# A gated feed-forward kernel behind a light convolution: the convolution laid on other steps, two of its taps moved from ScalarE and GpSimd to VectorE

## The chip, the cores and the metric

The kernel runs on one core of a Trainium2 chip. The metric is the device time of one execution in microseconds, as the median of several executions. All times below that belong to one place in the program come from one profiled execution.

## What is computed

The input x has 8 sequences of 4096 tokens with 192 channels. A causal convolution of 7 taps runs over the tokens; its weights are a softmax over the taps, one row for each of 8 groups of 24 channels. A feed-forward layer of width 2048 follows.

```
w   = softmax(weight)                     # 8 x 7, one row per group of 24 channels
y[t]= sum_k w[group, k] * x[t + k - 6]    # zeros ahead of a sequence
h   = y @ w_in                            # 32768 x 2048
g   = h            where h >= 1
      0            where h <= -1
      (h+1)^2 / 4  between
out = g @ w_out                           # 32768 x 192
```

Everything is float32. The kernel gets that precision from matmuls on values split into a high and a low part.

## The kernel before, in words

**Tiles.** The 32768 tokens are cut into 64 groups of TB = 512. A group goes through NPAIR = 8 steps, and a step handles two of the 16 slices of 128 hidden channels. So there are 512 steps q. Two groups, the tokens "a" (even group) and "b" (odd group), make a pair c; the 16 steps of a pair are called a block here, and i is the number of a step in its block. Steps 0 to 7 multiply a's tokens, 8 to 15 b's. Names: T is a transpose, R the rest.

**A step.** TensorE runs mm1(q), 18 matmuls that make h of this step, and then mm2(q-3), 18 matmuls that add g of three steps earlier into the four banks accm and accr. ScalarE makes relu and square (L570, L571) of h of this step and later the cast gh of the step before (L581). VectorE makes gl = g - gh of two steps before (L587), the sum m of gl's halves (L593), and g = max(h, min(g, 1)) of this step (L901), which frees h. h has two buffers, so mm1(q) needs g of q-2 to be done. Every eighth step, i = 2 and i = 10, ScalarE copies the four banks out (L617); GpSimd issues DMAs that add them up in the next two steps, and VectorE transposes the result (L639) in i = 7 and 8, and in 15 and 0.

**The convolution of the next groups runs beside this.** It works on three units: "a" (the first 128 channels of a's tokens), "b" (the same of b's), and "r", the rest (the last 64 channels of both). Each is loaded, transposed on VectorE (T, L164), and summed over taps 0 to 6. Method `taps` makes tap 0 on ScalarE and each later tap as a product on ScalarE (L238) and an addition on GpSimd (L249); `taps_dve` makes each as one fused operation of VectorE (L233). Before, only a uses `taps_dve` in the steady part. Then the unit is split into hi (a cast on ScalarE) and lo = y - hi: `split` subtracts on GpSimd (L280), `split_rest` on VectorE (L291). DMAs of SyncE's queue make copies of hi and lo with the halves of the partitions exchanged.

**What sets the order.** All engines run their queues in the order in which the program was written. The tables PLAN_B, PLAN_A and PLAN_R say in which step i which taps of a unit are written. The additions of GpSimd and its subtraction are held (`held`, `fresh`) and written one step after their product, with a dependency on the sum m of that step. mm1 of steps 0 to 7 reads a's hi and lo, that of steps 8 to 15 b's; r's are read in all 16. The blocks 0 and 1 have plans of their own (FIRST_A and the like; SECOND_B).

Of the kernel before, what the change touches and what calls it, by code (L numbers as in the profile page):

```python
# [8 lines left out]
F32 = mybir.dt.float32  # L9
# [22 lines left out]
def lightconv_then_ffn(ctx: ExitStack, tc: tile.TileContext, x, weight, w_in, w_out, out):  # L32
# [24 lines left out]
    nc = tc.nc  # L57
# [90 lines left out]
    class Conv:  # L148
# [137 lines left out]
        def split_rest(self):  # L286

            hi = xo.tile([P, TB], F32R, name="rh", bufs=2)
            lo = xo.tile([P, TB], F32R, name="rl", bufs=2)
            nc.scalar.copy(hi, self.y)  # L290
            nc.vector.tensor_sub(lo, self.y, hi.bitcast(F32))  # L291
            for key, t in (("hi", hi), ("lo", lo)):
                w = self.swapped(t, "r" + key, 2)
                xop[2 * self.c]["r", key] = (t[TOP], w[BOT])
                xop[2 * self.c + 1]["r", key] = (w[TOP], t[BOT])

        def split_halves(self):


            n = self.n  # L300
            y, late = self.y[:, 0:n], slice(n, TB)
            t, w = (act.tile([P, 2, TB], F32R, name=n, bufs=3) for n in ("gh", "gl"))
            t32, w32 = t.bitcast(F32), w.bitcast(F32)
            nc.scalar.copy(t[:, 0, 0:n], y)
            nc.vector.tensor_sub(t[:, 1, 0:n], y, t32[:, 0, 0:n])
            for to, half in ((t32[TOP, :, late], BOT), (w32[BOT, :, late], BOT),
                             (w32[BOT, :, 0:n], TOP)):
                nc.sync.dma_start(out=to, in_=t32[half, :, 0:n])
            for i, key in enumerate(("hi", "lo")):
                xop[2 * self.c + 1]["r", key] = (t[TOP, i], w[BOT, i])  # L310
# [497 lines left out]
    def whole(j, *cols):  # L808
        for _ in chunks[j].bits(*cols):
# [25 lines left out]

    PLAN_B = {12: ("T",), 14: (0, 1), 15: (2,), 0: (3,), 1: (4,), 2: (5,), 3: (6,), 5: "split"}
    PLAN_A = {1: ("T",), 2: (0,), 4: (1,), 6: (2,), 7: (3,), 9: (4,), 10: (5,), 11: (6,),
              12: "split"}  # L840
    PLAN_R = {2: ("T",), 4: (0,), 6: (1,), 7: (2,), 8: (3,), 9: (4,), 10: (5,), 11: (6,),
              13: "split"}
    SECOND_B = {0: (0, 1), 1: (2,), 2: (3,), 3: (4,), 4: (5, 6), 5: "split"}


# [5 lines left out]
    def conv_slot(i, b, a, r, turns=None):  # L851
        early = b is not None and b.c == 0
        plans = ((None if early else b, SECOND_B if b and b.c == 1 else PLAN_B),
                 (a, FIRST_A if early else PLAN_A),
                 (r, FIRST_R if early else PLAN_R))
        for u, plan in plans:
            what = plan.get(i, ()) if u else ()
            if turns is not None and turns != ("T" in what):
                continue
            if what == "split":  # L860
                if u is r:
                    u.split_rest()
                else:
                    u.split()
                continue
            if "T" in what:
                u.transpose()
            ks = [k for k in what if k != "T"]
            if ks:
                (u.taps_dve if u is a and not early else u.taps)(*ks)  # L870

# [60 lines left out]
    def first_step(q):  # L934
# [38 lines left out]
        if q > 6:  # L973
            advance(b, b)
        conv_slot(q, conv_b, conv_n.get("a"), conv_n.get("r"))

    conv_n, ahead = {}, {}
    for q in range(NQ + LATE):
# [10 lines left out]
        if c == 0 and i in (4, 5, 10):  # L989
            u = {4: "a", 5: "r", 10: "b"}[i]  # L990
# [18 lines left out]
        elif q < NF32:  # L1009
# [10 lines left out]
            act_max(q)  # L1020
            parts_lo(q, (False,))
            conv_slot(i, conv_b, conv_n.get("a"), conv_n.get("r"))
            if j >= NPAIR - 2:
                store(0, "mr"[j - NPAIR + 2])
        else:
# [17 lines left out]
            if q < NQ:  # L1043
                units = conv_b if i < 8 else conv_n.get("b"), conv_n.get("a"), conv_n.get("r")
                conv_slot(i, *units, turns=False)
# [55 lines left out]
```

## Time and profile before

| | |
|---|---|
| median of 3 runs | 2065.69 us (2064.97 to 2066.06) |
| the profiled execution | 2064.92 us |
| its span, first to last instruction | 2063.1 us |
| busy share of the span: TensorE, ScalarE, VectorE, GpSimd | 100%, 95%, 91%, 38% |
| granted TensorE clock, mean | 1.0 of full speed |

The busy share adds up the time in which at least one instruction of an engine was running; the ends of matmuls in it are modelled. A wait is shown in brackets behind the instruction that came after it, with the engine and line that ended it. A time from start to start of two neighbours on an engine is what the first one costs there; it can be shorter than the first one's own time, since they overlap.

### The profile page before, as it was taken

How to read it: one execution, taken by the hardware profiler on the slowest of the kernel's cores; microseconds unless marked ns; L12 is line 12 of the kernel's file. 1: busy time of each engine (PE TensorE's matmuls, PEld its weight loads, DVE VectorE, ACT ScalarE, POOL GpSimd, SP SyncE). 2: the span in 40 equal slices, each digit the busy share in tenths (PEclk: the TensorE clock that was granted, in tenths of full speed). 3: DMA queues.
4: the chain of work that ended last, by engine and by line, in shares of the span. 5: the costliest groups of instructions: out<-in, count | busy, mean ns of one | idle time of the engine just before them, and what ended most of it. 6: DMA issues, size and time to landing. Idle time of an engine off the chain costs nothing.

```text
span 2063.1 us, 46868 instructions
## 1 busy us (share of the span) xinstructions
PE 2054.3 (100%) x18644; PEld 1841.6 (89%) x18644; DVE 1871.6 (91%) x2109; ACT 1962.2 (95%) x2381; POOL 785.3 (38%) x749
## 2 busy tenths in 40 slices
PE   9999999999999999999999999999999999999999
PEld 6989889998899998888989998889899889998898
DVE  8898998999989999899899898998989989999988
ACT  7799999999999999999999999999999999999997
POOL 1534343343443433434434334344333343443431
PEclk9999999999999999999999999999999999999999
DMA  6333333443444434334333344343443433434323
GB/s 177 79 64 66 70 73 71 82 75 56 79 71 76 77 61 82 66 71 85 64 72 71 72 82 74 57 79 67 79 75 60 84 65 71 83 64 73 70 55 55
DMA packets 470685, 152.27 MB, mean 74 GB/s; under 512 B 418944, under 2 KB 426624, under 8 KB 470464
## 3 DMA queue, kind: packets, MB, share of 16 engines
q1 hardware_dynamic: 446880, 109.17, 25.9%
q0 software_dynamic: 23424, 39.99, 13.5%
q8 instruction: 146, 2.39, 0.5%
q14 instruction: 75, 0.61, 0.1%
q10 hardware_dynamic: 160, 0.10, 0.0%
HBM read 32.84 MB, written 25.17 MB: 28 GB/s over the span
## 4 chain that ended last, share of the span: by engine, by line
PE 67%; ACT 14%; DVE 9%; issue 4%; DMA 3%; POOL 2%; SPq 1%; ACTq 0%; DVEq 0%; POOLq 0%
PE h L483 34%; PE accr L536 20%; PE accm L536 10%; DVE gl L587 5%; ACT gh L581 4%; DMA lo<-lo 3%; ACT p L238 3%; ACT g L570 3%; ACT t L617 2%; POOL lo L280 2%; DVE g L901 2%; DVE y L233 1%; DVE m L593 1%; PE accm L503 1%; PE accr L503 1%
## 5 line engine op out<-in xcount | busy, mean ns | idle before, releaser
L587 DVE TENSOR_TENSOR gl<-g,gh 128x1024 fp32r<-128x1024 f32 x495 | 634.9, 1283 | 118.5 <-ACT gh L581 113.9
L536 PE MATMUL accr<-gh,wg 64*128 64x512 f32 x3960 | 635.9, 377 | 0.0
L483 PE MATMUL h<-hi,w 64*128 64x512 f32 x4032 | 634.2, 379 | 0.1
L901 DVE SCALAR_TENSOR_TENSOR g<-g,h 128x1024 f32<-128x1024 f32 x504 | 605.9, 1202 | 5.1 <-ACT g L571 3.0
L570 ACT ACTIVATE g<-h 128x1024 f32<-128x1024 f32 (+1 forms) x497 | 507.1, 1020 | 57.2 <-PE h L483 57.1
L571 ACT ACTIVATE g<-g 128x1024 f32<-128x1024 f32 (+1 forms) x497 | 525.8, 1058 | 15.8
L581 ACT CAST gh<-g 128x1024 fp32r<-128x1024 f32 x495 | 512.5, 1035 | 0.5 <-DVE g L901 0.4
L483 PEld LDWEIGHTS h<-hi,w 64*128 64x128 f32 x4032 | 418.6, 186 | 47.5 <-DVE g L901 12.5
L536 PEld LDWEIGHTS accr<-gh,wg 64*128 64x128 f32 x3960 | 406.5, 185 | 38.1
L483 PE MATMUL h<-lo,w 64*128 64x512 f32 x2016 | 435.1, 379 | 4.5 <-DMA lo<-lo 2.2
L249 POOL TENSOR_TENSOR y<-y,p 128x512 f32<-128x512 f32 x180 | 231.3, 1285 | 522.4 <-DVE m L593 269.0
L536 PE MATMUL accr<-gl,words 64*128 64x512 f32 x1980 | 419.0, 376 | 0.0
L249 POOL TENSOR_TENSOR r<-r,p 128x512 f32<-128x512 f32 x180 | 231.7, 1287 | 459.6 <-DVE m L593 269.5
L593 DVE TENSOR_TENSOR m<-gl 128x512 fp32r<-128x512 f32 x495 | 340.2, 687 | 26.7 <-PE h L483 0.5
L536 PE MATMUL accm<-gh,wg 64*128 64x512 f32 x1980 | 318.3, 376 | 0.0
L483 PE MATMUL h<-rhi,w 64*128 64x512 f32 x992 | 296.6, 379 | 0.0
L483 PE MATMUL h<-rh,w 64*128 64x512 f32 x992 | 293.6, 376 | 0.0
L483 PEld LDWEIGHTS h<-lo,w 64*128 64x128 f32 x2016 | 231.7, 186 | 40.1 <-DMA lo<-lo 24.5
L536 PEld LDWEIGHTS accr<-gl,words 64*128 64x128 f32 x1980 | 230.2, 186 | 16.2
L536 PEld LDWEIGHTS accm<-gh,wg 64*128 64x128 f32 x1980 | 215.2, 186 | 16.3
L627 POOL DMA_DIRECT2D t<-t x244 | 206.6, 983 | 31.3 <-ACT t L617 16.3
L536 PE MATMUL accm<-m,words 64*128 64x512 f32 x990 | 213.9, 382 | 0.0
(161 smaller groups left out, 2320.4 us busy)
## 6 DMA issues: line engine op xcount, KB each, us to landing
t<-t POOLq DMA_DIRECT2D x183, 128.0 KB, 3.6
out_dram<-osb SPq DMA_DIRECT2D x366, 64.0 KB, 1.9
raw<-in_x_dram SPq DMA_DIRECT2D x334, 68.0 KB, 2.6
hi<-hi SPq DMA_DIRECT2D x128, 128.0 KB, 3.1
lo<-lo SPq DMA_DIRECT2D x126, 128.0 KB, 2.3
t<-t POOLq DMA_DIRECT2D x61, 256.0 KB, 3.3
rhi<-rh SPq DMA_DIRECT2D x62, 128.0 KB, 3.1
rlo<-rl SPq DMA_DIRECT2D x62, 128.0 KB, 2.3
```

The costliest lines, as they stand in the source:

```text
L238: nc.scalar.mul(p, self.xT[:, SH + k:SH + k + TB], wk[:, self.wsel, k:k + 1])
L249: fresh.append(lambda p=self.product(k): nc.gpsimd.tensor_add(y, y, p))
L280: sub = eng.tensor_sub(lo, self.y, hi.bitcast(F32))
L483: nc.tensor.matmul(h[e], w[HALVES[e], c0:c0 + P], seen(x[e][e]), start=(n == 0), stop=(n == len(mms) - 1))
L536: mm = nc.tensor.matmul(accs[s][bank], w[half], in_turn(g[half]), start=(j == 0 and bank not in seen), stop=(j == NPAIR - 1 and k % 3 == 2 ...
L570: nc.scalar.activation(g[:, e, :], hs[q][:, e, :], AF.Relu, bias=0.5, scale=0.5)
L571: nc.scalar.activation(g[:, e, :], g[:, e, :], AF.Square)
L581: nc.scalar.copy(gh[:, e, :], gs[q][:, e, :])
L587: nc.vector.tensor_sub(gl[:, e, :], g[:, e, :], gh[:, e, :])
L593: return nc.vector.tensor_add(gt, gl[:, 0, :], gl[:, 1, :])
L627: nc.gpsimd.dma_start(out=to, in_=src, accum_op=ALU.add)
L901: nc.vector.scalar_tensor_tensor(out=g, in0=g, scalar=1.0, in1=h, op0=ALU.min, op1=ALU.max)
```

## The change

The three plans are laid out anew. The products and casts of ScalarE are taken off the steps 2 and 10, in which it copies the banks; B is transposed in step 10 and split in 3 (was 12 and 5), A is split in 11 (was 12), its taps 1 to 6 stand in steps 3 to 8 (were 4, 6, 7, 9, 10, 11). The rest's taps 5 and 6 become fused operations of VectorE in steps 9 and 10, and its split is written in two steps: the cast and hi's DMAs in step 12, the subtraction and lo's DMAs in step 13.

```diff
             nc.scalar.copy(hi, self.y)
-            nc.vector.tensor_sub(lo, self.y, hi.bitcast(F32))
             for key, t in (("hi", hi), ("lo", lo)):
+                if key == "lo":
+                    nc.vector.tensor_sub(lo, self.y, hi.bitcast(F32))
                 w = self.swapped(t, "r" + key, 2)
                 xop[2 * self.c]["r", key] = (t[TOP], w[BOT])
                 xop[2 * self.c + 1]["r", key] = (w[TOP], t[BOT])
+                yield
...
-    PLAN_B = {12: ("T",), 14: (0, 1), 15: (2,), 0: (3,), 1: (4,), 2: (5,), 3: (6,), 5: "split"}
+    PLAN_B = {10: ("T",), 11: (0,), 12: (1,), 13: (2,), 14: (3,), 15: (4,), 0: (5,), 1: (6,),
+              3: "split"}
...
+            if what in ("hi", "lo"):
+                if what == "hi":
+                    u.parts = u.split_rest()
+                next(u.parts)
+                continue
...
-                (u.taps_dve if u is a and not early else u.taps)(*ks)
+                dve = not early and (u is a or u is r and ks[0] > 4)
+                (u.taps_dve if dve else u.taps)(*ks)
```

VectorE's queue in the middle of a block, steps 9 and 10. Before, where y is a's sum and r the rest's tile:

```order
L587 TENSOR_TENSOR gl<-g,gh 128x1024
L233 SCALAR_TENSOR_TENSOR y<-xT,wk,y 128x512
L593 TENSOR_TENSOR m<-gl 128x512
L901 SCALAR_TENSOR_TENSOR g<-g,h 128x1024
L587 TENSOR_TENSOR gl<-g,gh 128x1024
L233 SCALAR_TENSOR_TENSOR y<-xT,wk,y 128x512
L593 TENSOR_TENSOR m<-gl 128x512
L901 SCALAR_TENSOR_TENSOR g<-g,h 128x1024
```

And of the changed kernel in the same two steps:

```order
L589 TENSOR_TENSOR gl<-g,gh 128x1024
L233 SCALAR_TENSOR_TENSOR r<-r,wk 128x512
L595 TENSOR_TENSOR m<-gl 128x512
L910 SCALAR_TENSOR_TENSOR g<-g,h 128x1024
L589 TENSOR_TENSOR gl<-g,gh 128x1024
L233 SCALAR_TENSOR_TENSOR r<-r,wk 128x512
L595 TENSOR_TENSOR m<-gl 128x512
L164 STREAM_TRANSPOSE xT<-raw 128x544
L910 SCALAR_TENSOR_TENSOR g<-g,h 128x1024
```

The taps in these steps are the rest's now, a's have moved ahead of them, and B's transpose has come from step 12 into step 10.

ScalarE's queue in steps 11 to 13, right behind the copies of the banks. Before:

```order
L570 ACTIVATE g<-h 128x1024
L571 ACTIVATE g<-g 128x1024
L238 ACTIVATE p<-r,wk 128x512
L581 CAST gh<-g 128x1024
L570 ACTIVATE g<-h 128x1024
L571 ACTIVATE g<-g 128x1024
L275 CAST hi_14028<-y 128x512
L581 CAST gh<-g 128x1024
L570 ACTIVATE g<-h 128x1024
L571 ACTIVATE g<-g 128x1024
L290 CAST rh<-r 128x512
L581 CAST gh<-g 128x1024
```

Of the changed kernel, steps 11 and 12 and the start of 13:

```order
L572 ACTIVATE g<-h 128x1024
L573 ACTIVATE g<-g 128x1024
L245 ACTIVATE y<-xT,wk 128x512
L275 CAST hi_13926<-y 128x512
L583 CAST gh<-g 128x1024
L572 ACTIVATE g<-h 128x1024
L573 ACTIVATE g<-g 128x1024
L238 ACTIVATE p<-xT,wk 128x512
L290 CAST rh<-r 128x512
L583 CAST gh<-g 128x1024
L572 ACTIVATE g<-h 128x1024
```

The casts hi of A and rh of the rest have come a step nearer to the copies, and stand with B's first two taps. VectorE's subtraction rl stays in step 13.

GpSimd's queue from the rest's first addition to B's last. Before:

```order
L249 TENSOR_TENSOR r<-r,p 128x512 x5
L627 DMA t<-t 128x512
L627 DMA t<-t 64x512
L249 TENSOR_TENSOR r<-r,p 128x512
L627 DMA t<-t 64x512 x2
L280 TENSOR_TENSOR lo_1862<-y,hi_1861 128x512
L249 TENSOR_TENSOR y<-y,p 128x512 x5
L627 DMA t<-t 128x512
L627 DMA t<-t 64x512
L249 TENSOR_TENSOR y<-y,p 128x512
L627 DMA t<-t 64x512 x2
L280 TENSOR_TENSOR lo_2388<-y,hi_2387 128x512
```

Of the changed kernel:

```order
L249 TENSOR_TENSOR r<-r,p 128x512 x4
L629 DMA t<-t 128x512
L629 DMA t<-t 64x512
L280 TENSOR_TENSOR lo_1812<-y,hi_1811 128x512
L629 DMA t<-t 64x512 x2
L249 TENSOR_TENSOR y<-y,p 128x512 x6
L629 DMA t<-t 128x512
L629 DMA t<-t 64x512
L280 TENSOR_TENSOR lo_2280<-y,hi_2279 128x512
L629 DMA t<-t 64x512 x2
```

The rest has four additions instead of six, and each subtraction lo now stands between the two halves of the DMAs that add up the banks.

## Rows read from the trace of the kernel before

**Rows 1.** Page, part 1: busy time of each engine, share of the span, instructions.

```profile
PE 2054.3 (100%) x18644; PEld 1841.6 (89%) x18644; DVE 1871.6 (91%) x2109; ACT 1962.2 (95%) x2381; POOL 785.3 (38%) x749
```

**Rows 2.** Chain of waits, last block: start, length, work; first and last of 16.

```profile
1989.93 1.94 PE h L483 x18
...
2048.20 1.83 PE h L483 x12
```

**Rows 3.** Timeline of TensorE, first mm1 of two successive blocks: start, length, instructions.

```profile
909.56 0.59 PE L483 MATMUL h<-hi,w 64*128 64x512 f32 x4
...
973.06 0.59 PE L483 MATMUL h<-hi,w 64*128 64x512 f32 x4
```

**Rows 4.** Timeline, step 8 of that block, with GpSimd's subtraction in step 6.

```profile
938.35 1.28 POOL L280 TENSOR_TENSOR lo<-y,hi 128x512 fp32r<-128x512 f32 x1 [4.02 <-ACT p L238]
...
940.64 0.59 PE L483 MATMUL h<-hi,w 64*128 64x512 f32 x4
...
942.49 0.18 PEld L483 LDWEIGHTS h<-lo,w 64*128 64x128 f32 x1 [0.44 <-DMA lo<-lo]
...
945.29 0.70 PE L483 MATMUL h<-hi,w 64*128 64x512 f32 x4
```

**Rows 5.** List of waits: who waited for whom, us in total, times, longest.

```profile
DVE rl L291 <- ACT rh L290: 25.7, 31, 1.0
PEld h L483 <- DMA lo<-lo: 24.5, 59, 0.5
```

**Rows 6.** Timeline, steps 13 to 15 of the block before that one.

```profile
902.46 0.60 ACT L290 CAST rh<-r 128x512 fp32r<-128x512 f32 x1
...
902.96 1.04 ACT L581 CAST gh<-g 128x1024 fp32r<-128x1024 f32 x1
...
903.09 0.69 DVE L291 TENSOR_TENSOR rl<-r,rh 128x512 fp32r<-128x512 f32 x1 [0.82 <-ACT rh L290]
...
903.70 0.69 DVE L593 TENSOR_TENSOR m<-gl 128x512 fp32r<-128x512 f32 x1
...
904.44 0.19 PEld L536 LDWEIGHTS accm<-m,words 64*128 64x128 f32 x2 [0.34 <-DVE m L593]
...
905.57 0.30 PEld L483 LDWEIGHTS h<-hi,w 64*128 64x128 f32 x4 [0.40 <-DVE g L901]
```

**Rows 7.** Timeline of ScalarE, step 2 and the start of step 3.

```profile
919.48 1.03 ACT L570 ACTIVATE g<-h 128x1024 f32<-128x1024 f32 x1 [0.23 <-PE h L483]
...
921.50 1.05 ACT L617 COPY t<-accr 128x512 f32<-128x512 f32 x2
...
923.40 0.75 ACT L238 ACTIVATE p<-xT,wk 128x512 f32<-128x512 f32 x1
924.03 1.05 ACT L581 CAST gh<-g 128x1024 fp32r<-128x1024 f32 x1
924.96 1.04 ACT L570 ACTIVATE g<-h 128x1024 f32<-128x1024 f32 x1
```

**Rows 8.** Timeline of VectorE, steps 6, 7 and 12, and mm1 of step 14.

```profile
935.72 1.23 DVE L587 TENSOR_TENSOR gl<-g,gh 128x1024 fp32r<-128x1024 f32 x1
936.86 0.75 DVE L233 SCALAR_TENSOR_TENSOR y<-xT,wk,y 128x512 f32<-128x512 f32 x1
937.53 0.68 DVE L593 TENSOR_TENSOR m<-gl 128x512 fp32r<-128x512 f32 x1
938.13 1.22 DVE L901 SCALAR_TENSOR_TENSOR g<-g,h 128x1024 f32<-128x1024 f32 x1
939.28 1.43 DVE L587 TENSOR_TENSOR gl<-g,gh 128x1024 fp32r<-128x1024 f32 x1
...
962.80 0.74 DVE L164 STREAM_TRANSPOSE xT<-raw 128x544 f32<-128x544 f32 x1
963.46 1.18 DVE L901 SCALAR_TENSOR_TENSOR g<-g,h 128x1024 f32<-128x1024 f32 x1
...
964.72 0.70 PE L483 MATMUL h<-hi,w 64*128 64x512 f32 x4
```

More of the change, by code (lines that the diff above doesn't have):

```diff
@@ L833, in lightconv_then_ffn @@
     whole(2, 0, CI)
-    PLAN_B = {12: ("T",), 14: (0, 1), 15: (2,), 0: (3,), 1: (4,), 2: (5,), 3: (6,), 5: "split"}
[L839 to L842, printed above, removed]
+    PLAN_B = {10: ("T",), 11: (0,), 12: (1,), 13: (2,), 14: (3,), 15: (4,), 0: (5,), 1: (6,),
+              3: "split"}
+    PLAN_A = {1: ("T",), 2: (0,), 3: (1,), 4: (2,), 5: (3,), 6: (4,), 7: (5,), 8: (6,), 11: "split"}
+    PLAN_R = {2: ("T",), 3: (0,), 4: (1,), 5: (2,), 6: (3,), 7: (4,), 9: (5,), 10: (6,), 12: "hi",
+              13: "lo"}
     SECOND_B = {0: (0, 1), 1: (2,), 2: (3,), 3: (4,), 4: (5, 6), 5: "split"}
@@ L859, in conv_slot @@
                 continue
+            if what in ("hi", "lo"):
[3 more added lines that the diff above has]
+                continue
             if what == "split":
                 if u is r:
-                    u.split_rest()
+                    for _ in u.split_rest():
+                        pass
                 else:
```

## The prediction, made before the changed kernel was run

> **What bounds the kernel now.** TensorE is busy for 100% of the span, ScalarE 95%, VectorE 91%, GpSimd 38% [rows 1]. That share does not say whether TensorE waits, since the ends of its matmuls are modelled, so I read its pace instead. In the last block of 16 steps, which has nearly no convolution, the chain of waits is TensorE alone; from its first mm1 to its sixteenth it takes 58.27 us, which is 3.885 us a step [rows 2]. That is what the 36 matmuls of a step need, and the change leaves them alone: sixteen steps cannot take less than 62.16 us. A block in the middle takes 973.06 - 909.56 = 63.50 us [rows 3], so each of the 29 blocks 2 to 30 (alike within 0.4 us) loses 1.34 us, 38.9 us in all. This is what a better order can win.
>
> Where a block loses it: (a) **Step 8** takes 945.29 - 940.64 = 4.65 us, 0.77 too many; TensorE waits for the DMA that lands lo of the tokens B [rows 4]. Its source is GpSimd's subtraction in step 6, from the split that PLAN_B puts in step 5. The list of waits has this wait 59 times, two a block [rows 5]. (b) **Steps 14 and 15** lose the other 0.57. In step 13 VectorE stands 0.82 us before rl, because ScalarE's cast rh is still to come; the sum m and the maximum g stand behind rl in its queue. TensorE then waits 0.34 for m, and later 0.40 until g is made and h is free [rows 6]. The wait for rh occurs 31 times [rows 5].
>
> **Taking (a) away.** B's split moves from step 5 to step 3, its subtraction from 6 to 4: two paces, 7.77 us, earlier, where 0.77 are missing. With T(n) for the start of mm1 of step n, it starts at about T(4)+6.05 (0.8 after m, as in [rows 4, 8]), and with the 2.9 us from its end to the weight load that it lets go [rows 4] its data are there more than 5 us before step 8 reads them. Gain 29 x 0.77 = 22.3 us. A's split goes from 12 to 11, which only adds slack.
>
> **Taking (b) away.** The cast of the rest's hi stands in step 12 and the subtraction in 13, so VectorE finds rh made; y of the rest is complete in step 10. Gain 29 x 0.57 = 16.6 us, if nothing else makes VectorE late there.
>
> **ScalarE.** From start to start, relu and square cost 2.02 us, the four copies of an evacuation 1.90, a product 0.63, the cast gh 0.93 [rows 7], a cast of one half 0.50 [rows 6]. A step without extras is 2.95, which is 0.93 under the pace. Before, steps 2 and 10 hold copies and a product, 1.60 over. Now they hold the copies alone: 0.97 behind. Step 11 (cast, first tap) and step 12 (cast, product) lose 0.20 each, so it is 1.37 behind at worst; the five steps 13 to 1, one product each, give 0.30 back apiece, which just fits before step 2. After step 2 it is 0.97 behind, after step 3 1.17, and back on pace in step 7. A block has two products fewer, 2 x 0.63 = 1.26 us, and ScalarE needs 60.1 in it (16 x 2.95 + 12 x 0.63 + 3 x 0.50 + 2 x 1.90). That wins nothing by itself, since TensorE is the bound; it keeps the lag under the old one. GpSimd loses two additions of 1.28 a block, and nobody waits for them.
>
> **VectorE is where a price may stand.** From start to start a fused tap takes 0.67 us, gl 1.14, m 0.60, g 1.15, a transpose 0.66 [rows 8]; a step with a tap is 3.56. It gets two taps more a block (2 x 0.67 x 30 = 40 us of work), and since A's taps are moved together and R's stand behind them, each of the steps 3 to 10 has a tap, and 7, 8 and 10 a transpose too. Additions of the rest in steps 5 and 6, and B's subtraction in 4, run into the next gl: it took 1.43 instead of 1.23 with GpSimd's lo beside its start [rows 4, 8], so 0.20 more in steps 5, 6 and 7. In step 4 gl starts 3.44 after T(4), when ScalarE's cast of step 3 is done (relu at 2.15 after T, that is 919.48 less 909.56 + 2 x 3.885 [rows 3, 7]; 0.97 late; + 2.02 + 1.13, a cast of 1.03, 0.02, - 3.885). From there VectorE has no gap. Start of gl after T: step 5 3.14, step 6 3.02, step 7 2.89, step 8 3.40, step 9 3.70, step 10 3.38. End of g after T: step 8 3.40 + 1.14 + 0.67 + 0.60 + 0.63 + 1.21 = 7.65 (the half transpose put at 0.63), step 10 3.38 + 1.14 + 0.67 + 0.60 + 0.66 + 1.21 = 7.66. The limit is two paces less 0.08, 7.69: g frees the h that mm1 wants two steps on, and in step 12 of before g ended at 964.64 and that mm1 started at 964.72 [rows 8]. So the stretch ends with 0.03 us to spare, by a sum of ten terms. Steps 11 to 15 hold few extras and bring VectorE back. I take 0.1 us a block lost here (30 x 0.1 = 3 us), between 0 and 0.5 (15 us; 0.5 is 0.1 more on each of five taps). Below zero it can't go, since TensorE sets the pace.
>
> **The rest.** Block 1 keeps SECOND_B, so its steps 3 to 5 hold B's taps and now R0, R1, R2 besides, and ScalarE comes out about 1 us later than now: once, between 0 and 3 us; I take 2. R's tap in step 9 has a new wait, on GpSimd's last addition. That one starts at T(8)+5.9 to 6.1, ends by T(8)+7.4, and the tap is due at T(8)+8.7; behind it stand m and g of step 9. It costs nothing while those 1.3 us last. B's transpose in step 10 reads data that were loaded in step 0.
>
> **Sum.** The profiled execution's 2064.92 (span 2063.1 and 1.8 around it) - 38.9 + 3 + 2 = 2031.0; the median of the runs lies 0.8 above it: 2031.8, said as 2032.
>
> **Rivals.** *VectorE becomes the bound of steps 3 to 10.* For it speaks the margin of 0.03 us; against it, that a step with a tap (3.56, or 3.76 beside GpSimd) is still under the pace. If each of the three meetings with GpSimd cost the whole 0.35 us that its subtraction had left when gl began [rows 4, 8], and not 0.20, a block would lose 0.45 more: 2032 + 30 x 0.4 = 2044. The Trainium skill has such a rule: its page "SBUF — State Buffer", section "Who interferes with whom", says that a VectorE instruction with two SBUF inputs is blocked fully behind a GpSimd one that started first. By that rule the time is this rival's; the row agrees that gl is held up, but shows 0.20 of the 0.35. Chance 0.18.
>
> *Only the first stall goes.* If VectorE is still late in step 13, (b) stays: 2032 + 16.6 = 2048. For it speaks that gl there waits for ScalarE's cast of step 12, which now has two operations ahead of it; against it, that m would end at T(13)+6.1 (3.64 + 1.14 + 0.6 + 0.7), where it ended at 7.06 (904.39, and T(13) = 964.72 - 63.50 - 3.885). Chance 0.10.
>
> *Slower.* If R's tap in step 9 waits for GpSimd, VectorE's queue stands behind it. Were that addition a whole step late (3.885), each block would lose 3.885 - 1.3 = 2.6 and win 1.34: 2066 + 30 x 1.2 = 2102. It decides from 2.7 us of lateness on (1.3 + 1.34). GpSimd began 0.8 after m in the rows, so 0.04.
>
> *The loss moves.* TensorE's waits in steps 8 and 14 give ScalarE and VectorE time to come up; without them the lag may stop TensorE elsewhere, by as much, and the time stays 2066. Against it, ScalarE has 2.1 us a block to spare: 0.06.
>
> **How the numbers follow.** Forecast 0.62 (2026 to 2037, 2032 likeliest), VectorE bound 0.18 (2044), half the gain 0.10 (2048), no change 0.06, slower 0.04. A measurement of this kernel tells some 0.2% (4 us) from no change. The low end is the whole gain at no cost, 2065.7 - 38.9 = 2026.8, less 2 for block 1's own small loss; the high end takes in the VectorE case: 2047. Faster 0.90, same 0.06, slower 0.04.
>
> **What would show it.** TensorE's wait for DMA lo and VectorE's wait for rh should go from the list, and a block should take 62.2 to 62.4 us. If VectorE is the bound, TensorE waits for g at the start of mm1 in steps 10 to 12. If the wait for m in step 14 remains, the cast of rh was not its cause. The prediction is wrong if VectorE waits for GpSimd's r in step 9, or if blocks stay above 63 us.

## The result, and the profile after

The changed kernel takes 2035.8 us (2035.5 to 2036.34, 4 runs) against 2065.42 of the kernel before in the same comparison: a ratio of 0.986, 95% interval 0.984 to 0.987. That is 29.6 us, or 1.4%, faster. The prediction said 2032 and a range of 2025 to 2047. The profiled execution took 2035.54 us, its span is 2033.8.

The page of the changed kernel, part 1, answers to [rows 1] (busy time, share of the span, instructions):

```profile
PE 2027.6 (100%) x18644; PEld 1766.5 (87%) x18644; DVE 1902.7 (94%) x2169; ACT 1920.5 (94%) x2321; POOL 708.9 (35%) x689
```

VectorE has 60 instructions more and 31 us more of busy time, ScalarE 60 fewer, GpSimd 60 fewer. TensorE's share reads 100% as before, though from step 5 of block 1 on it lost 40 us to waits then and 11 now: here the share does not see them. The pace does. The first mm1 of two successive blocks (start, length), as in [rows 3]:

```profile
898.52 0.59 PE L485 MATMUL h<-hi,w 64*128 64x512 f32 x4
...
960.98 0.60 PE L485 MATMUL h<-hi,w 64*128 64x512 f32 x4
```

A block takes 62.46 us; it was 63.50, and TensorE's pace alone gives 62.16. Each of the blocks 2 to 30 now loses 0.31, where it lost 1.3 to 1.7 (the 29 of them lost 39.7 us in the trace of before, and lose 9.0 now). Of the two waits in [rows 5] the one for DMA lo has gone from the list, and that for rh is left once, in an early block. This is the list of waits of the changed kernel (who waited for whom, us in total, times, longest):

```profile
PEld h L485 <- DVE g L910: 14.3, 33, 0.5
...
DVE rl L293 <- ACT rh L290: 1.0, 1, 1.0
```

What is left from block 2 on is one wait a block for g, at mm1 of step 10. The timeline of steps 7 to 10 shows how it comes about (start, length, instruction):

```profile
931.32 0.70 DVE L641 STREAM_TRANSPOSE osb<-t 128x512 f32<-128x512 f32 x1
931.95 1.18 DVE L910 SCALAR_TENSOR_TENSOR g<-g,h 128x1024 f32<-128x1024 f32 x1
...
933.05 1.20 DVE L589 TENSOR_TENSOR gl<-g,gh 128x1024 fp32r<-128x1024 f32 x1
...
933.48 0.59 PE L485 MATMUL h<-hi,w 64*128 64x512 f32 x4
...
934.84 0.68 DVE L595 TENSOR_TENSOR m<-gl 128x512 fp32r<-128x512 f32 x1
...
935.55 0.71 DVE L641 STREAM_TRANSPOSE osb<-t 64x512 f32<-64x512 f32 x1
...
936.29 1.22 DVE L910 SCALAR_TENSOR_TENSOR g<-g,h 128x1024 f32<-128x1024 f32 x1
...
937.57 0.30 PEld L485 LDWEIGHTS h<-hi,w 64*128 64x128 f32 x4 [0.44 <-DVE g L910]
```

mm1 of step 9 starts at 933.48, so T(8) is 929.60 and mm1 of step 10 was due at 937.37. VectorE has no gap between two of its instructions here; g of step 8 starts at 936.29 and ends at 937.51, 7.91 after T(8), and mm1 of step 10 starts at 937.57, 0.20 late. After that stop step 10 takes 0.10 too long as well: its second pair of matmuls starts 0.32 us after the first, where it is 0.22 in step 9.

### The profile page after: what moved, and what is told of

Same layout as the page of the kernel before. It is cut to its first block, busy times and chain, and to the rows that moved or that the text cites. A ratio compares the mean times of both kernels' runs of the same rounds, so it can differ in the third digit from the quotient of the medians.

```text
span 2033.8 us, 46783 instructions
## 1 busy us (share of the span) xinstructions
PE 2027.6 (100%) x18644; PEld 1766.5 (87%) x18644; DVE 1902.7 (94%) x2169; ACT 1920.5 (94%) x2321; POOL 708.9 (35%) x689
## 4 chain that ended last, share of the span: by engine, by line
PE 96%; DVE 2%; ACT 1%; issue 1%; DMA 0%; SPq 0%; DVEq 0%; POOL 0%; ACTq 0%; POOLq 0%
PE h L485 48%; PE accr L538 30%; PE accm L538 15%; PE accm L505 1%; DVE gl L589 1%; PE accr L505 1%; DVE g L910 1%; DVE m L595 0%; ACT gh L583 0%; DMA out_dram<-osb 0%; PE accr L215 0%; ACT t L619 0%; DVE y L233 0%; ACT g L572 0%; DVE osb L641 0%
## 5 line engine op out<-in xcount | busy, mean ns | idle before, releaser
L538 PE MATMUL accr<-gh,wg 64*128 64x512 f32 x3960 | 589.8, 376 | 0.0
L485 PEld LDWEIGHTS h<-hi,w 64*128 64x128 f32 x4032 | 383.0, 186 | 64.6 <-DVE g L910 14.3
L538 PEld LDWEIGHTS accr<-gh,wg 64*128 64x128 f32 x3960 | 373.7, 185 | 53.7
L485 PE MATMUL h<-lo,w 64*128 64x512 f32 x2016 | 386.3, 376 | 0.0
L538 PE MATMUL accr<-gl,words 64*128 64x512 f32 x1980 | 376.2, 376 | 0.1
L249 POOL TENSOR_TENSOR r<-r,p 128x512 f32<-128x512 f32 x120 | 154.1, 1284 | 259.6 <-DVE m L595 259.6
L485 PEld LDWEIGHTS h<-lo,w 64*128 64x128 f32 x2016 | 194.7, 186 | 26.0
L538 PEld LDWEIGHTS accr<-gl,words 64*128 64x128 f32 x1980 | 187.8, 186 | 26.6 <-DVE gl L589 0.5
L538 PEld LDWEIGHTS accm<-gh,wg 64*128 64x128 f32 x1980 | 187.8, 186 | 26.0
L485 PEld LDWEIGHTS h<-rhi,w 64*128 64x128 f32 x992 | 184.7, 186 | 13.1
```

The lines of the kernel that those rows point to most:

```text
L249: fresh.append(lambda p=self.product(k): nc.gpsimd.tensor_add(y, y, p))
L485: nc.tensor.matmul(h[e], w[HALVES[e], c0:c0 + P], seen(x[e][e]), start=(n == 0), stop=(n == len(mms) - 1))
L538: mm = nc.tensor.matmul(accs[s][bank], w[half], in_turn(g[half]), start=(j == 0 and bank not in seen), stop=(j == NPAIR - 1 and k % 3 == 2 ...
```

## The experiments

Two readings were to be told apart. Mine: each loss has a place of its own (lo of B in step 8; VectorE's wait for rh in step 13; now VectorE's row of taps up to step 8). The rival: TensorE loses time because ScalarE lags after copying the banks, and only ScalarE's load counts.

### The rest's split alone

The kernel before, with the cast in step 13 and the subtraction in 14:

```diff
-              13: "split"}
+              13: "hi", 14: "lo"}
```

> The kernel before, with one thing changed: the cast of the rest's hi in step 13, the subtraction lo in step 14 (both were in 13). Theory: VectorE's wait for the cast is all of the loss in steps 14 and 15, 0.57 us in each of 29 blocks; it goes, the loss of step 8 stays: 2065.4 - 16.6 = 2049, steps 14 and 15 at 3.89 us, step 8 still about 4.66. Rival: the loss there is ScalarE's lag after the copies of step 10, and the wait for the cast only marks it; then 2062 to 2066.

Measured: 2050.3 us (ratio 0.993, 0.992 to 0.995), against 2049. Steps 14 and 15 lose 0.08 us instead of 0.57, step 8 still 0.8. The wait for rh is not in its list of waits, the one for lo still is:

```profile
PEld h L485 <- DMA lo<-lo: 24.7, 58, 0.6
```

So the wait of VectorE was the cause of (b), at ScalarE's full old load.

### The new table of the tokens B alone

The kernel before with PLAN_B of the change, all else as it was.

> The kernel before, with the new table for the tokens B alone: transposed in step 10, taps in 11 to 1, split in 3. Theory: the loss of step 8 goes (29 x 0.77 = 22 us), but ScalarE now has B's first taps besides the rest's last ones in steps 11 to 13 and is 2.3 us behind there instead of 1.6; the cast rh then ends at about T(13)+7.5 instead of 5.7, VectorE waits for it, and steps 14 and 15 lose some 2 us more a block: 2065 - 22 + 29 x 1.9 = about 2098, between 2075 and 2105. Rival: the moves are independent of each other and this one brings its 22 us, 2043.

Measured: 2115.4 us, slower by 50 (ratio 1.024, 1.023 to 1.026); 17 more than expected, and above the range given. Step 8 is at TensorE's pace, so that loss is gone here too. But steps 14 and 15 lose 2.6 us, in three blocks 4.1, and step 0 up to 0.8 besides. In the list of waits VectorE stands 1.9 us for rh, and TensorE for m:

```profile
PEld accm L536 <- DVE m L593: 70.6, 57, 2.2
...
DVE rl L291 <- ACT rh L290: 58.1, 31, 1.9
PE accm L536 <- DVE m L593: 53.6, 30, 1.8
```

The direction and the place were right. Of the excess over the forecast, 8 us are lost in steps 0 to 2, and 4.4 in the three blocks. There TensorE's clock fell. These are two neighbouring stretches of the first of them, block 2 (length, busy time and instructions of TensorE, its weight loads, VectorE, ScalarE and GpSimd, granted clock, the DMAs' share and GB/s):

```profile
207.20:210.60 3.40, 1.68 (x14) 1.17 (x16) 3.02 (x4) 3.37 (x5) 1.58 (x2) 1.00 0.74 151
210.60:214.00 3.40, 3.40 (x20) 2.71 (x18) 3.30 (x3) 1.65 (x3) 2.68 (x2) 0.50 0.28 66
```

Behind the wait for m, in which TensorE was busy for half of the time, the granted clock is 0.50 for 3.4 us (1.2 instead of 2.4 GHz), and step 15 loses 1.79 us, not 0.32; blocks 10 and 21 show the same. Why the wait was followed by this in three blocks and not in the other 26, the runs don't tell. What wins 22 us in company costs 50 alone: B's first taps in steps 11 to 13 make the cast rh later, and VectorE stands until it is made.

### The rest's split together again

The changed kernel with cast and subtraction both in step 13:

```diff
-    ... 10: (6,), 12: "hi",
-              13: "lo"}
+    ... 10: (6,),
+              13: "split"}
```

> The changed kernel, with the rest's split undone to one step: cast and subtraction both in 13. Theory: VectorE waits for rh again; it stands behind a product of B there and ends at T(13)+6.3, 0.5 later than in the kernel before, so steps 14 and 15 lose about 1.1 us a block: 2036 + 30 x 1.1 = 2069, between 2058 and 2072. Rival: with ScalarE less behind (the copies stand alone in step 10) the order of the split doesn't matter, 2036 to 2040.

Measured: 2069.1 us (ratio to the kernel before 1.002, 1.001 to 1.003), as expected: with this one step undone all of the change's gain is gone, and more. Steps 14 and 15 lose 1.01 and 0.10 in each block. The timeline of step 13, with ScalarE's product p and cast rh, VectorE's rl and m, and TensorE's weight load for m:

```profile
969.13 0.70 ACT L238 ACTIVATE p<-xT,wk 128x512 f32<-128x512 f32 x1
969.75 0.60 ACT L290 CAST rh<-r 128x512 fp32r<-128x512 f32 x1
...
970.38 0.69 DVE L293 TENSOR_TENSOR rl<-r,rh 128x512 fp32r<-128x512 f32 x1 [1.90 <-ACT rh L290]
970.99 0.68 DVE L595 TENSOR_TENSOR m<-gl 128x512 fp32r<-128x512 f32 x1
...
971.73 0.19 PEld L538 LDWEIGHTS accm<-m,words 64*128 64x128 f32 x2 [0.98 <-DVE m L595]
```

VectorE had 1.90 us of nothing to do ahead of rl, and m, which needs neither rl nor rh, stood behind it.

### The rest's two taps back on ScalarE and GpSimd

The changed kernel with its tables, but without the condition that puts taps 5 and 6 of the rest on VectorE:

```diff
-                dve = not early and (u is a or u is r and ks[0] > 4)
+                dve = not early and u is a
```

> The changed kernel with the same tables, but the rest's taps 5 and 6 made by ScalarE and GpSimd again, in steps 9 and 10. Theory: ScalarE has the product in step 10 with the copies and two products more a block, so it is up to 2.0 us behind after step 12 and still 0.5 behind in step 2; VectorE's chain of taps begins 0.4 later in step 4 and g of step 8 comes 0.4 later, and m and g of step 13 come close to their limits: 0.31 us lost a block becomes 0.8 to 1.1, 2036 + 30 x 0.6 = 2054, between 2046 and 2062. Rival: the two taps are worth nothing as ScalarE is not the bound, and the tables do it all: 2034 to 2038.

Measured: 2047.4 us (ratio 0.992, 0.990 to 0.993). The forecast was 2054, within 2046 to 2062. A block loses 0.68 us instead of 0.31: 0.33 and 0.10 in steps 9 and 10, and 0.14 and 0.10 in 14 and 15, at both places that were named. The two taps alone are thus worth 11.6 us of the change, not by ScalarE being the bound but by its lag: gl of step 4 starts 0.13 us later, and m of step 13 ends 0.59 us later, after T (6.71 instead of 6.12, medians over the blocks).

### The transpose over all partitions

The changed kernel, with the transpose of the second half of a result on 128 partitions instead of the lower 64:

```diff
-        nc.vector.transpose(out=osb[n].rearrange("p j b -> p (j b)"), in_=y[n])
+        nc.vector.transpose(out=osb.rearrange("p j b -> p (j b)"), in_=y)
```

> The changed kernel, with one thing changed: the transpose of the second half of a result (steps 8 and 0) covers all 128 partitions instead of the lower 64; the same DMAs store the lower 64. Theory: in step 8 the half transpose cost VectorE 0.22 more than the whole one in step 7, since it began only when m had ended and g only when it had ended (1.45 us from the start of m to that of g, against 1.24). With the whole one g of step 8 ends 0.22 sooner, at T(8)+7.70, which is at the limit of 7.72: of the 0.31 us a block 0 to 0.1 stays, 2036 - 30 x 0.26 = 2028, between 2026 and 2031. Rival: the half transpose begins late because it waits for its DMAs, then nothing changes, 2035 to 2037.

Measured: 2028.1 us (ratio 0.982, 0.981 to 0.984), against 2028: 7.7 us for twice the rows. A block loses 0.04. The timeline of VectorE in step 8:

```profile
931.64 0.68 DVE L595 TENSOR_TENSOR m<-gl 128x512 fp32r<-128x512 f32 x1
932.24 0.70 DVE L641 STREAM_TRANSPOSE osb<-t 128x512 f32<-128x512 f32 x1
932.87 1.18 DVE L910 SCALAR_TENSOR_TENSOR g<-g,h 128x1024 f32<-128x1024 f32 x1
```

From the start of m to that of g it is 1.23 us, where the half one of the changed kernel took 1.45 (934.84 to 936.29 above). The half one began when m had ended, and g began when it had ended; the whole one overlaps with both. It is not a wait for its DMAs, as those are the same. The half one lies on partitions 64 to 127; whether it is their number or their place that keeps it from overlapping, no run here tells.

### No tap in step 8, and two taps in step 8

The changed kernel with A's tap 6 and the rest's taps 5 and 6 each one step later, and, the other way, with the rest's taps in 8 and 9:

```diff
-    PLAN_A = {... 7: (5,), 8: (6,), 11: "split"}
+    PLAN_A = {... 7: (5,), 9: (6,), 11: "split"}
...
-    PLAN_R = {... 7: (4,), 9: (5,), 10: (6,), 12: "hi",
+    PLAN_R = {... 7: (4,), 10: (5,), 11: (6,), 12: "hi",
```

```diff
-    PLAN_R = {... 7: (4,), 9: (5,), 10: (6,), 12: "hi",
+    PLAN_R = {... 7: (4,), 8: (5,), 9: (6,), 12: "hi",
```

> The changed kernel with A's tap 6 in step 9 and the rest's taps 5 and 6 in steps 10 and 11 (each one step later), so that step 8 has a transpose alone. Theory: VectorE saves 0.5 us ahead of g of step 8 (0.66 for the tap, less about 0.15 since m then follows gl at once), g ends at T(8)+7.4, and the loss of 0.31 us a block goes; steps 10 and 11 have the room: 2036 - 9 = 2027, between 2025 and 2030. Rival: TensorE's wait in step 10 has another cause than VectorE's row of taps, 2034 to 2037.

> The changed kernel with the rest's taps 5 and 6 in steps 8 and 9 (were 9 and 10): VectorE has two taps and a transpose in step 8. Theory: VectorE has no slack in step 8, so the whole tap, 0.67 us, is seen at mm1 of step 10: a block loses 0.31 + 0.67 = 0.98, 2036 + 30 x 0.67 = 2056, between 2053 and 2060. Rival: VectorE is not what steps 9 and 10 wait for, 2035 to 2040.

Measured: 2026.5 us (ratio 0.982, 0.980 to 0.983) without a tap in step 8, 2055.3 (ratio 0.996, 0.994 to 0.997) with two; 2027 and 2056 were expected. Without it no block from 2 on loses anything. With two, a block loses 0.97, and TensorE's waits for g are those of step 10 again, at the weight load and at the matmul:

```profile
PEld h L485 <- DVE g L910: 33.8, 33, 1.1
PE h L485 <- DVE g L910: 20.5, 29, 0.7
```

VectorE's stretch to step 8 is the one place where the changed kernel still loses time from block 2 on: a tap more there costs all of its 0.66 us, a tap less wins no more than the 0.31 that is lost.

### Without the rest's additions on GpSimd

The changed kernel without GpSimd's additions of taps 1 to 4 of the rest (its output lacks those taps):

```diff
-                    fresh.append(lambda p=self.product(k): nc.gpsimd.tensor_add(y, y, p))
+                    p = self.product(k)
+                    if self.u != "r":
+                        fresh.append(lambda p=p: nc.gpsimd.tensor_add(y, y, p))
```

> The changed kernel without GpSimd's additions of the rest's taps 1 to 4 (their products are still made by ScalarE and used by nobody, so the rest lacks these taps). Theory: gl of steps 6 and 7 (and 14, 15 are untouched) takes 1.22 instead of 1.46 and 1.48, g of step 8 ends 0.45 sooner, and no block loses anything: 2036 - 9 = 2027. Rival: the longer gl is no part of the loss since VectorE has the time, 2034 to 2036.

Measured, in a single execution: 2025.5 us, against 2027; no block from 2 on loses anything. gl of steps 6 and 7 in the changed kernel, and then without the additions:

```profile
924.86 1.46 DVE L589 TENSOR_TENSOR gl<-g,gh 128x1024 fp32r<-128x1024 f32 x1
...
928.65 1.48 DVE L589 TENSOR_TENSOR gl<-g,gh 128x1024 fp32r<-128x1024 f32 x1
```

```profile
920.02 1.21 DVE L591 TENSOR_TENSOR gl<-g,gh 128x1024 fp32r<-128x1024 f32 x1
...
923.54 1.22 DVE L591 TENSOR_TENSOR gl<-g,gh 128x1024 fp32r<-128x1024 f32 x1
```

The 0.25 us in each come from GpSimd, and this too is enough to take the loss away. The stretch is a sum; whichever term goes, some 0.25 us suffices. Another 0.7 us is won in step 7 of block 1, which loses 0.10 here and 0.84 in the changed kernel.

### All together, and block 1

The changed kernel with both cures for step 8 (no tap in it, the whole transpose), and a plan of its own for the rest in block 1:

```diff
+    SECOND_R = {2: ("T",), 4: (0,), 6: (1,), 7: (2,), 8: (3,), 9: (4,), 10: (5,), 11: (6,), 12: "hi",
+                13: "lo"}
...
-                 (r, FIRST_R if early else PLAN_R))
+                 (r, FIRST_R if early else SECOND_R if b and b.c == 1 or r and r.c == 2 else PLAN_R))
```

> The changed kernel with no tap in step 8, the whole transpose, and in block 1 alone the rest's product taps where they were before the change (steps 4, 6, 7, 8, 9; taps 5 and 6 on VectorE in 10 and 11). Theory: the 2.1 us that block 1 loses in steps 6 to 8 come from ScalarE, which has B's last taps and the rest's first ones at once there; with them apart again block 1 loses at most 0.3, and with the rest of the stalls gone the kernel runs at TensorE's pace: 2026.5 - 2 = 2024.5, between 2024 and 2026. Rival: block 1 loses its time for another reason (GpSimd's additions right behind each other), 2026 to 2027.

Measured: 2026.1 us (2026.1 to 2026.49; ratio 0.981, 0.980 to 0.982), the rival's number. The kernel before took 2065.7 us beside this run and 2064.6 beside the one without a tap in step 8, so a difference of 1 us or so between these runs tells nothing by itself; the trace decides. Block 1 still loses 1.67 us in steps 5 to 7, where the changed kernel loses 2.07 in steps 6 to 8, and the kernel before lost 0.47, in steps 14 and 15. (Its steps 0 to 4 lose another 4.5 us or so in all three; they are left aside here.) The timeline there, GpSimd's two additions of B's last taps, then B's subtraction, with VectorE's m beside them and TensorE's weight loads that wait:

```profile
105.50 3.04 POOL L251 TENSOR_TENSOR y<-y,p 128x512 f32<-128x512 f32 x2 [2.27 <-ACT p L238]
110.13 1.34 POOL L280 TENSOR_TENSOR lo<-y,hi 128x512 fp32r<-128x512 f32 x1 [1.58 <-ACT hi L275]
...
105.63 1.77 DVE L595 TENSOR_TENSOR m<-gl 128x512 fp32r<-128x512 f32 x1
...
110.25 1.77 DVE L595 TENSOR_TENSOR m<-gl 128x512 fp32r<-128x512 f32 x1
...
107.45 0.19 PEld L538 LDWEIGHTS accm<-m,words 64*128 64x128 f32 x2 [0.80 <-DVE m L595]
...
112.07 0.19 PEld L538 LDWEIGHTS accm<-m,words 64*128 64x128 f32 x2 [0.60 <-DVE m L595]
```

m takes 1.77 us instead of 0.68, twice. In block 1 B's additions are not held until the sum m is done, as they are from block 2 on, so they start where they hurt: with ScalarE relieved its products are made sooner, and the additions begin at 105.50, where they begin at 106.78 in the changed kernel.

So this is another loss than that of the changed kernel, and it does not refute my theory of block 1. There VectorE's gl of step 5 stands for ScalarE's cast gh. Before, and in the changed kernel:

```profile
107.88 1.67 DVE L587 TENSOR_TENSOR gl<-g,gh 128x1024 fp32r<-128x1024 f32 x1 [0.80 <-ACT gh L581]
```

```profile
108.83 1.68 DVE L589 TENSOR_TENSOR gl<-g,gh 128x1024 fp32r<-128x1024 f32 x1 [1.16 <-ACT gh L583]
```

mm1 of step 5 starts at 104.17 and at 104.06, so gl is 1.06 us later than before, and step 6 loses 1.12. That is ScalarE's load, as expected. The 0.84 us of step 7 are GpSimd's, since they go with the rest's additions. What was wrong is that relieving ScalarE would suffice: it uncovers a loss of nearly the same size. A version that also holds B's additions there was not tried; at most 1.7 us are to be had in these steps.

## Why the prediction was right, and where a term was off

**The bound and the size of the gain.** TensorE's pace of 3.885 us a step was the bound, and 1.34 us a block all that could be won. The mean block lost 1.37 us, a little more than the 1.34 of the one that was read (39.7 us in all, not 38.9). The kernel without a tap in step 8 runs every block from 2 on at that pace, and takes 2026.5 us. That the prediction had its free end so near, at 2026.8, is partly luck: it left out 0.8 us of gain and 1.6 us that block 1 costs.

**(a) and (b)** went as said: steps 8, 14 and 15 take 3.88 us in the changed kernel, and m of step 13 ends 6.12 us after T, where the sum said 6.1. That their causes were the late lo and the cast in front of rl, and not ScalarE's lag as such, is shown by the split apart (2050.3), the split together (2069.1) and B's table alone, in which step 8 is cured while ScalarE lags more than ever. The changed kernel shows it too: relu of step 13 starts 3.56 us after T, later than before (3.12), and steps 14 and 15 lose nothing.

**ScalarE.** By the sums it is 1.37 us behind at worst, at the start of step 13; the 3.56 us of relu in step 13 are 1.41 later than on pace. That the two products are worth nothing by themselves holds only as long as the lag stays short: with them back the kernel is 11.6 us slower.

**VectorE, the term that was mis-sized.** The place was named to the step: g of step 8, 0.03 us to spare, a wait of TensorE for g at mm1 of step 10. The price taken was 0.1 us a block; it is 0.31, which is 9.0 us instead of 3. The step that failed is "the half transpose put at 0.63". From the start of m over the half transpose to the start of g I had 0.60 + 0.63 = 1.23; it takes 1.45. Of the 0.26 us by which g of step 8 ends later than the sum said (7.91, not 7.65), 0.22 are this, and 0.05 were there when gl of step 8 began. mm1 of step 10 is 0.20 late by it; the other 0.10 of the 0.31 are lost in step 10 behind the stop, a cost that the sum did not have. With the whole transpose the 1.23 are right, and so is the forecast of 2028. The same three instructions stand in step 8 of the kernel before, 1.46 from m to g, so a row that I had could have told:

```profile
944.94 0.69 DVE L593 TENSOR_TENSOR m<-gl 128x512 fp32r<-128x512 f32 x1
945.66 0.71 DVE L639 STREAM_TRANSPOSE osb<-t 64x512 f32<-64x512 f32 x1
946.40 1.22 DVE L901 SCALAR_TENSOR_TENSOR g<-g,h 128x1024 f32<-128x1024 f32 x1
```

(Two slips in the arithmetic change nothing: gl of step 5 starts at 3.44 + 3.56 - 3.885 = 3.12, not 3.14, and 30 x 0.45 would put the rival of 2044 at 2045.5.)

**Block 1** cost 1.6 us more than before (2.07 - 0.47), where 2 were taken. The reason given, ScalarE about 1 us later, is there (1.06) and stands behind the larger part; the 0.84 us of step 7 are GpSimd's, which the prediction did not have.

**The sum** in the measured terms: 2064.92 - 39.7 + 9.0 + 1.6 = 2035.8, and the profiled execution took 2035.54. Of the rivals, VectorE as the bound came to its place at a smaller price than its 2044. Slower by a wait in step 9 for GpSimd's r did not occur: that wait is not in the list.

**The rule weighed.** The prediction read gl's 0.20 us beside GpSimd's last 0.35 as less than what the Trainium skill's page "SBUF — State Buffer", section "Who interferes with whom", says, namely that the second one is blocked until the first has finished. The traces agree with the page, but for a fixed part. In the last run's block 1 m began when the addition beside it had 1.22 us left, and took 1.09 longer than its 0.68; in the changed kernel gl of step 6 met 0.38 and took 0.25 longer. Of the 118 times that gl or m meets a running GpSimd addition or subtraction with more than 0.2 us left, between 100 and 1900 us of the changed kernel's trace, each loses what is left less 0.12 to 0.13. So the 0.20 of 0.35 were the full hold, less this part; and the rival's 0.45 a block, which took all of the 0.35 three times, was too much by about this part each time.

## What to carry to other kernels

Where the bound engine shows 100% busy, take its pace from a stretch that is surely undisturbed and compare step by step; the lost time then has an address, and the instruction that waits there, with what is queued behind it, is a better guide than any engine's share. Split a hand-over between two in-order engines into two steps, so that the receiver never finds it unmade: the same work in the same step cost 33 us here. And before work is moved to an engine with little slack, add up its starts up to each deadline from pairs of rows that show just the pair in question; a stretch with 0.03 us to spare has none.

## What the runs showed of the hardware that I had not expected

- VectorE's transpose of 64 partitions takes as long as one of 128 (0.71 and 0.70 us), and the one here, on partitions 64 to 127, does not overlap with its neighbours of 128 partitions: 0.71 and 0.74 us from start to start where the whole one has 0.60 and 0.63. Making it twice as large saved 7.7 us.
- A VectorE instruction with both inputs in SBUF that starts while a GpSimd addition runs takes longer by all that the addition has left, less 0.13 us: m took 1.77 us instead of 0.68. In block 1 of the changed kernel gl took 2.33 instead of 1.22, beside two GpSimd instructions right behind each other:

```profile
111.39 1.52 POOL L280 TENSOR_TENSOR lo<-y,hi 128x512 fp32r<-128x512 f32 x1 [1.97 <-ACT hi L275]
112.87 1.27 POOL L249 TENSOR_TENSOR r<-r,p 128x512 f32<-128x512 f32 x1
...
112.90 2.33 DVE L589 TENSOR_TENSOR gl<-g,gh 128x1024 fp32r<-128x1024 f32 x1
```

- A stop of TensorE at the first weight load of mm1 costs 0.10 us on top of itself: after the wait at the start of mm1 in step 10 that step took 3.99 us instead of 3.885, in all of the 29 blocks, and so did step 15 of the kernel before.
